# Sparse attention and a gated FFN on one core: the keys loaded first, a PSUM unit for zero matmuls, all early blocks in halves, a new order

## The chip, the cores and the metric

The kernel runs on one core of a Trainium2 chip. The metric is the device time of one execution in microseconds; lower is better. It is given as the median of several runs, and one execution more is taken with the hardware profiler.

## The reference

Four sequences of 768 tokens with 8 heads of 64 go through block-sparse attention (blocks of 32; a query block sees its neighbours, the first and last block, and three sampled blocks), and the result through a gated FFN of width 1536. Cut to what is computed:

```python
scores = (1 / np.sqrt(D)) * np.matmul(q, k.transpose(0, 1, 3, 2))
scores = np.where(mask, scores, -1000000000.0)       # mask: window, first/last, sampled blocks
attn = np.exp(scores - scores.max(-1, keepdims=True))
attn = attn / (attn.sum(-1, keepdims=True) + 1e-09)
x = np.matmul(attn, v)                               # -> 3072 tokens x 512
gate = 1.0 / (1.0 + np.exp(-(x @ w_gate)))
out = (gate * (x @ w_val)) @ w_out
```

## The kernel before

The work is cut into 12 units of 256 queries: three for each sequence (batch). A unit has four pairs of heads. For each pair there are three **score** steps (256 keys each): PE multiplies the transposed keys kT by the queries qT, two heads side by side in the two halves of its rows, ACT takes the exponential of the 128x1024 result into P, and for all units but the first DVE multiplies P by a 0/1 mask. In unit 0 the mask isn't ready as a tile in time; there a **bias** is added by extra matmuls, so a score step has eight matmuls instead of four. Then **PV**: 24 products of P and the values (with a column of ones for the sums), a reciprocal and a multiplication on DVE, and **xt**, the transpose of the result (units 0 and 1 on PE, the later ones by a transposing DMA on SP's queue).

The FFN follows by groups: units 0 to 3 each alone, then two at a time. A group has **F** blocks (x by w_gate and w_val into the two banks of one PSUM unit, tanh on ACT, the product on DVE into ht) and **y** parts (ht by w_out), a copy and a store. A group of one unit has six F blocks; each needs x from all four pairs and one of the six parts of w_gate and w_val.

PSUM is four units of two banks. Every task that writes PSUM takes a unit, and the order says which.

A block can be done in two ways. `whole` contracts 128 rows at a time. `turns` works with the two 64-row halves of the array side by side: in the first half-task the upper rows write bank 0 and the lower ones bank 1, in the second they change banks, and the second starts with a wait for the last matmul of the first. `WIDE = 2` makes PV and F whole in units 0 and 1. The closing blocks of the last unit (`y_last`) are whole in any case.

**The order.** Each piece of work is added to a list and gets a number; `ORDER`, written out by hand, says in which order they are issued, and each engine runs its own in that order. `30:2` is task 30 in PSUM unit 2; a letter (A or D) gives the copy to ACT or DVE; `215@30` issues load 215 after task 30 has run; `j3` is a pair of zero matmuls into unit 3, 64 rows by 512 columns each (L315). At the start of `ORDER` the numbers mean: 0 the block mask on DVE; 1 and 2 the bias, 3 and 4 the mask rows; 5 to 13 the casts, transposes and copies of pair 0's keys and queries; 15 to 18 transposes and copies of pair 1; 30 to 65 scores and PVs of unit 0; 66 to 73 the queries' later tiles; the F blocks of the first group begin with 126.

**Loads.** The first keys and queries come as float32 on SP's and ACT's queues (`first_heads`, L247) into a staging tile and are cast; the constants (identity and the mask's table) come on SP's queue, `e64` (which spreads block values over positions) by two loads. All else of batch 0 and the weights comes on POOL's queue, in the order of `FIRST`: k, q, v of the later pairs (k1 is the keys of pair 1; q1 the first queries of pair 1), then r0 to r3 (the later queries of the pairs) between w0 to w5 (parts of w_gate and w_val), at last o0 to o2 (w_out).

```python
nc.sync.dma_start(const, const_h.ap())
nc.scalar.dma_start(sbi, sampled_blocks)
first_heads(nc.sync, k32, k, 0, NT)
first_heads(nc.scalar, q32, q, 0, 2)
nc.gpsimd.dma_start(e64[0:NB], spread_h.ap())
nc.scalar.dma_start(e64[D : D + NB], spread_h.ap())
```

Of the kernel before, what the change touches and what calls it, by code (L numbers as in the profile page):

```python
# [21 lines left out]
NB = S // BLK  # L22
# [19 lines left out]
23D 25:3 27:2 37 26D 215@30 50:1 28D 46:3 51 82:2 48:0 83D 47 64:1 49 84:2 60:0 85D 65 38:3 29 61  # L42
56:2 39 66:1 57 42:0 67D 54:3 43D 52:1 165:0 53D 55 93:2 24 58:1 166 94 99:3 59 68:2 95:0 100 96D
181:1 69D 62:0 182 63D 78:3 102:2 162:0 79D 144@102 103 70:1 126:3 125@50 71D 183 163 164 111:1
127 119:2 131:0 120 128 167 112 104 138:3 122:2 132 145:1 123 133 121 139 124 169:0 146 140 147
72:2 170 86:3 159:1 73D 87 171 152:2 160 205:0 153 108:3 88 89:1 206 105@89 90 101 174:2 92@165
154 109 187@89 207 239:1 91 235@86 175 155:0 188:3 110 156 114@40 176 168@155 240 113 115:0 157
189 141:2 116 202:1 142 190 195:0 203 143 196 232:3 172:2 233 129:0 173 97:3 191:2 130 204 192A
193 98A 117:0 256 212:2 194 216 118A 213 184:3 177:0 217 178A 185 134:2 148:0 218 149D 135D 241
242:0 198:3 221A 252:2 214 199 136 179 219A 258 180 246:3 200 253 227 137 254 268:1 247 257 243  # L50
248 150 229:2 234 151 269 209:3 300:0 210 270 259 161 230 237 197 293:1 296:3 228 301 284:2 231
297 302 238 244 294 280:0 186 287:3 285 201@280 211 281 286 249:1 298 288 277:0 223:2 289 278 250
224 251 336:3 327:0 337 158@336 225 274 264:1 279 261:2 271:3 265 295 236 328 262 266 272 310:1
329 273 311 226 263 307:2 320:3 255 340 308 290 312 303:1 321 309 323:2 341 282 324 333:3 208 304
378@333 322 342 334 305 347:2 345A 343D 351:3 314:1 245@351 352 348 338 372:0 315 299@64 349 373
365:3 316 357@181 369 375:2 353 386:0 403@239 358:1 376 317 374 366 387 377 325 354:2 359 367 355
368 404:0 360 356 432:3 400:2 405 433 361 313@400 260 393:1 326@307 401 335 411:3 267@333 406 402
418:2 394 419 424@418 412 407 283@138 395 362:0 413 389:2 379:1 390 414 363 397:3 425:2 364 398
# [3 lines left out]
442:3 385 448 493:2 457A 451 455A 443 371 516:1 465 494 517 444 507:0 429 430 495 518 459:3 490:1  # L62
# [3 lines left out]
532:2 644:0 551 533 529:1 645 534 597:2 562 530 646 563 557 598 594:0 564 578 392@594 595 531  # L66
601:1 633@421 565D 567A 561@32 627:2 569:0 610 628 573:3 579@141 570 602 438@122 571 574 629
339@555 630:2 587:0 631 596 704@50 647:3 575 588 548@397 603 648 604 600@470 580:2 396 683@209 589
662:1 545:3 581 668@165 663 590 632 619:0 546 622:1 664 582 599 620 611:3 623 583 612 621 615:2
624 665:3 625 673:0 666 616 547 350 674 756:1 614@40 634:3 675 757 710 695 584:0 553 617 635 445  # L70
718@435 618 651:1 636 535@662 585 650@102 680:2 652 586 681 637 684:0 653 613 677:2 701:3 654 685
# [3 lines left out]
739:0 727 733 679 731 743:3 740 744 734 741 755 688:1 752 735A 722:0 728 689 737A 723 690 787:3  # L75
749:2 788 724 801:1 572 742 798:0 745 790:3 750 799 748 709 751 791 766:0 541 802 792 769:3 759
770 711 772:1 767 760 773 768 676 844:3 779:0 761 775:1 762A 764D 845 780 763 818:2 776 781 800
# [6 lines left out]
906 916 885 912 909A 921:1 913 974 946 922 924 927 923 907D 970:3 941:2 900 931 971 901:0 942 972  # L84
918:3 932 917 919 933 902 947:2 934D 954:3 936A 975 903 959:0 965:1 960 943 948 961 955 949 966
# [6 lines left out]
1067:0 1065 1081 1068 1085 1069 937 1066 1070 1086 935 1074 910 1075 1087 1076 1090D 1100:3 1091  # L92
1079D 1096:0 1077D 1078 1101 1080 1097 1102 1132:2 1103 1098 1088A 1108:3 1099 1089 1120:1 1109
1112:0 1110 1121 1111 1113 1122 1092:3 1123 1114 1124:1 1115 1133 1093 1104:0 1094 1125 1095 1105
1126 1134 1136:3 1127 1106 1135 1116:1 1107 1128:2 1117 1137 1118 1129 1119 1138 1140:0 1139 1130
1141 1131 1142 1150:1 1151 1152 1143 1153 1144 1154 1145 1160:3 1146A 1148D 1161 1147 1162 1149
1155:2 1163 1156 1164 1157 1158 1159
"""
GAP, PV_HALF, F_HALF, Y_ONE = 0.3, 0.36, 0.875, 0.216
WIDE = 2  # L100
# [20 lines left out]
class Plan:  # L121
# [13 lines left out]
    def run(self):  # L135
        done = set()
        for token in self.order:
            if token[0] == "j":
                self.idle(int(token[1:]))
# [15 lines left out]
def kernel(  # L155
# [46 lines left out]
    e64 = sing.tile([128, S], f16)  # L202
    nc.vector.memset(e64, 0.0)
# [47 lines left out]

    nc.sync.dma_start(const, const_h.ap())
# [32 lines left out]
    junk = sing.tile([128, 512], f16)  # L285
    nc.vector.memset(junk, 0.0)
# [816 lines left out]
```

## Time and profile before

| | us |
|---|---|
| median of 3 runs | 283.47 (283.11 to 285.92) |
| the profiled execution | 281.96 |
| its span, first to last instruction | 280.2 |
| PE busy in it | 272.4 (97%) |
| ACT / DVE / POOL busy | 192.1 / 187.9 / 47.4 |

PE is TensorE's matmuls, PEld its weight loads (they overlap with matmuls), DVE VectorE, ACT ScalarE, POOL GpSimd, SP SyncE. Timeline rows give the start, the duration, engine and line, what is written and read, shape and count, and in brackets the idle time before it with what ended it; neighbours of one kind are merged, and the duration of a merged row goes from its first start to its last end. Matmuls overlap: what one costs is seen from the start of the next, not from its duration. Rows of DMA issues give the size of one and the time from issue to landing.

### The profile page before, as it was taken

How to read it: one execution, taken by the hardware profiler on the slowest of the kernel's cores; microseconds unless marked ns; L12 is line 12 of the kernel's file. 1: busy time of each engine (PE TensorE's matmuls, PEld its weight loads, DVE VectorE, ACT ScalarE, POOL GpSimd, SP SyncE). 2: the span in 40 equal slices, each digit the busy share in tenths (PEclk: the TensorE clock that was granted, in tenths of full speed). 3: DMA queues.
4: the chain of work that ended last, by engine and by line, in shares of the span. 5: the costliest groups of instructions: out<-in, count | busy, mean ns of one | idle time of the engine just before them, and what ended most of it. 6: DMA issues, size and time to landing. Idle time of an engine off the chain costs nothing.

```text
span 280.2 us, 10875 instructions
## 1 busy us (share of the span) xinstructions
PE 272.4 (97%) x4889; PEld 186.1 (66%) x4889; DVE 187.9 (67%) x387; ACT 192.1 (69%) x239; POOL 47.4 (17%) x70
## 2 busy tenths in 40 slices
PE   5999999999999999999999999999999999999995
PEld 2677786777899799766555655666656667555543
DVE  4667894788887888688778746875664888142421
ACT  3798888699897878898668866578677683023301
POOL 8975441011531000082400000000000000000000
PEclk9799999999999999999999999999999999999999
DMA  7999999765589975279967330041100012440003
GB/s 148 184 195 196 200 205 202 110 127 87 77 110 150 206 129 126 40 106 188 125 115 162 68 97 2 12 133 50 30 2 0 6 21 65 117 180 2 0 5 147
DMA packets 56679, 28.92 MB, mean 103 GB/s; under 512 B 33044, under 2 KB 53676, under 8 KB 56632
## 3 DMA queue, kind: packets, MB, share of 16 engines
q0 software_dynamic: 21552, 13.93, 35.6%
q1 hardware_dynamic: 34592, 13.99, 22.7%
q8 instruction: 38, 0.62, 0.9%
q10 hardware_dynamic: 488, 0.30, 0.4%
q14 instruction: 9, 0.07, 0.1%
HBM read 28.47 MB, written 6.29 MB: 124 GB/s over the span
## 4 chain that ended last, share of the span: by engine, by line
PE 91%; DMA 3%; ACT 2%; DVE 2%; issue 1%; SPq 0%; DVEq 0%
PE m L338 89%; DMA xT<-x 2%; DMA e<-bb_spread 1%; ACT P L570 1%; PE m L456 1%; DVE ysb L833 1%; ACT ysb L831 0%; PE m L451 0%; DVE kT L282 0%; DVE mask L282 0%; ACT mask L280 0%; SPq L667 0%; PE m L397 0%; DVE x L616 0%; PE m L315 0%
## 5 line engine op out<-in xcount | busy, mean ns | idle before, releaser
L570 ACT ACTIVATE P<-m 128x1024 f16<-128x1024 f32 x144 | 142.5, 1025 | 31.3 <-PE m L338 27.3
L338 PE MATMUL m<-xT,wv 64*128 64x512 f16 (+2 forms) x672 | 136.1, 331 | 0.3 <-issue 0.3
L338 PE MATMUL m<-xT,wg 64*128 64x512 f16 (+2 forms) x672 | 135.9, 331 | 0.1
L576 DVE TENSOR_TENSOR P<-P,mask 128x1024 f16<-128x1024 f16 x132 | 86.7, 686 | 11.1 <-ACT P L570 10.8
L338 PEld LDWEIGHTS <-wg 64*128 64x128 f16 (+1 forms) x672 | 61.8, 94 | 20.5 <-issue 2.0
L338 PEld LDWEIGHTS <-wv 64*128 64x128 f16 (+1 forms) x672 | 61.8, 94 | 15.9 <-issue 0.3
L338 PE MATMUL m<-wo,ht 64*128 64x512 f16 (+2 forms) x564 | 70.7, 372 | 0.0
L765 DVE SCALAR_TENSOR_TENSOR ht<-th,m 128x512 f16<-128x512 f32 x72 | 49.0, 686 | 30.6 <-ACT th L762 29.6
L762 ACT ACTIVATE th<-m 128x512 f32<-128x512 f32 x72 | 42.7, 598 | 36.0 <-PE m L338 35.3
L338 PE MATMUL m<-qT,kT 64*128 64x256 f16 x576 | 54.0, 272 | 0.3 <-DVE ysb L833 0.2
L338 PEld LDWEIGHTS <-P 64*128 64x128 f16 (+1 forms) x2112 | 46.2, 94 | 9.0 <-issue 1.1
L338 PE MATMUL m<-vex,P 64*128 64x65 f16 (+1 forms) x2112 | 48.2, 190 | 0.0
L338 PEld LDWEIGHTS <-ht 64*128 64x128 f16 (+1 forms) x564 | 30.5, 94 | 21.6 <-issue 1.3
L338 PEld LDWEIGHTS <-kT 64*128 64x128 f16 x576 | 27.4, 95 | 13.0 <-issue 1.7
L220 POOL DMA_DIRECT2D v<-in_v_dram x16 | 11.4, 717 | 65.3 <-PE m L338 56.5
L616 DVE TENSOR_TENSOR x<-m,rz 128x256 f16<-128x256 f32 x48 | 20.4, 425 | 1.7
L615 DVE RECIPROCAL rz<-m 128x4 f32<-128x4 f32 x48 | 8.7, 180 | 17.9 <-PE m L338 16.4
L220 POOL DMA_DIRECT2D q<-in_q_dram x19 | 13.6, 723 | 12.1 <-PE m L338 11.1
L831 ACT ACTIVATE ysb<-m 128x512 f32<-128x512 f32 x13 | 7.5, 597 | 10.6 <-PE m L338 9.9
L833 DVE TENSOR_SCALAR ysb<-m 128x512 f32<-128x512 f32 x9 | 6.1, 688 | 11.8 <-ACT ysb L831 5.5
L220 POOL DMA_DIRECT2D k<-in_k_dram x15 | 10.8, 723 | 6.1 <-PE m L338 5.5
L338 PE MATMUL m<-bias,e 64*128 64x256 f16 x48 | 6.9, 301 | 0.3
(46 smaller groups left out, 69.7 us busy)
## 6 DMA issues: line engine op xcount, KB each, us to landing
out_dram<-ysb SPq DMA_DIRECT2D x23, 256.0 KB, 2.4
v<-in_v_dram POOLq DMA_DIRECT2D x16, 192.0 KB, 5.5
k<-in_k_dram POOLq DMA_DIRECT2D x15, 192.0 KB, 5.9
q<-in_q_dram POOLq DMA_DIRECT2D x12, 192.0 KB, 7.1
wg<-in_moe_w_gate_dram POOLq DMA_DIRECT2D x6, 256.0 KB, 8.6
wv<-in_moe_w_val_dram POOLq DMA_DIRECT2D x6, 256.0 KB, 8.9
wo<-in_moe_w_out_dram POOLq DMA_DIRECT2D x3, 512.0 KB, 12.8
xT<-x SPq DMA_TRANSPOSE x40, 3.2
```

Source lines behind the costliest of these rows:

```text
L220: return nc.gpsimd.dma_start(dst[:, h0:h1, t0:t1, :], src[b, h0:h1].rearrange("h (p t) d -> p h t d", t=NT)[:, :, t0:t1, :],)
L338: return nc.tensor.matmul(out, lhsT, rhs, start=start, stop=stop, skip_group_check=True).ins
L456: nc.tensor.transpose(out16[a * D : (a + 1) * D, h, i * D : (i + 1) * D], tile_[rows, a], ident[rows, rows],)
L570: nc.scalar.activation(self.pt.rearrange("a h i n -> a (h i n)"), both(self.bank).rearrange("a h n -> a (h n)"), AF.Exp, bias=0.0, scale=SCALE
L576: nc.vector.tensor_tensor(self.pt, self.pt, m.unsqueeze(1).broadcast_to([128, 2, 2, UQ]), op=ALU.mult,)
L615: nc.vector.reciprocal(rz, self.acc[:, :, :, D : D + 1])
L616: nc.vector.tensor_tensor(self.x16.rearrange("a s h d -> a h s d"), self.acc[:, :, :, 0:D], rz.broadcast_to([128, 2, 2, D]), op=ALU.mult,)
L762: nc.scalar.activation(th, both(bank)[:, 0, :], AF.Tanh, bias=0.0, scale=0.5)
L765: nc.vector.scalar_tensor_tensor(self.ht[:, tiles[0] : tiles[-1] + 1, :], in0=th.rearrange("a (f n) -> a f n", n=self.w), scalar=1.0, in1= ...
L831: nc.scalar.activation(ysb, both(bank)[:, s, :], AF.Copy, bias=0.0, scale=0.5)
L833: nc.vector.tensor_scalar(ysb, in0=both(bank)[:, s, :], scalar1=0.5, scalar2=None, op0=ALU.mult)
```

## The change

The order of the loads: the first keys go ahead of the constants on SP's queue, and `e64` comes on SP's queue (behind the constants) and on POOL's. The tile of zeros is smaller, cleared before `e64`, and read with a repeated axis; beside `j3` there is `j3s`, a pair of 128 columns, and the zero matmuls run on in unit 3 between the first real pieces. The block mask (task 0) is issued after the casts of the keys instead of ahead of everything, reads the sampled blocks without a cast, and reduces once into both places. `WIDE` and `WIDE_PV` are 0: PV and F of units 0 and 1 are in halves too, 20 tasks more (1185 for 1165), so the numbers are others. `EARLY` is 0, so the branch that it guards isn't taken. `ORDER` is another from first to last. In the new numbers, 15 to 18 are still pair 1's transposes and copies; 69, 71, 73 and 75 are the transposes of the later queries (r0 to r3) of pairs 0 to 3; 96 and 97 are unit 0's last PV; 93, 90, 113, 116, 104 are exponentials of unit 1; 131 is the first half of the first F block.

```diff
+EARLY = 0
 ORDER = """
-j3 j3 j3 j3 0 j3 j3 j3 11D 1:0 8A 3:1 5D 12:2 6:3 4A 7D 2 13A 80:3 106:1 9:0 30:2 107A 10D 81D
-15:1 31 34:0 16D j3 76:3 17:2 35 32:1 18D 77D 74:2 33 40:0 14 20:3 75D 41 44:1 21D 22:2 45 19 36:0
...
+j3 j3 j3 j3 j3 j3 j3 5A 8D j3 j3s j3s 0 j3s j3s 9:0 j3s j3s 11A 10D j3s 1:1 j3s j3s j3s 12:2 2 3:0
+13A 6:1 j3s 32:2 4D 7A 15:1 17:3 33 34:0 18D 16D 122:3 35 77:2 123D 30:1 78D 31 81:3 45:0 82D 22:2
+46 36:1 23D 41:3 37 20:2 21D 25:0 42 19 52:1 26D 56:2 53 47:3 14 49:0 57 38:1 48 27:2 50 28D 39
+51 63:2 58:3 24 64 83:0 40 84D 101:1 59 67:2 29 102A 69:0 60:3 68 70D 71:1 43:0 61 72A 44D 92:2
+89:0 62 93 112:1 54:3 55D 90 79:2 73:3 80D 113 115:0 74D 96:2 87:3 116 97 88D 103:1 98 104 65:3
+124:0 66D 99:2 146:3 125 100D 75:1 114 131:2 147 76D 106:0 117 127:1 132 107 126 194:3 128 138:0
...
-WIDE = 2
+WIDE, WIDE_PV = 0, 0
...
+    junk = sing.tile([128, 128], f16)
+    nc.vector.memset(junk, 0.0)
     nc.vector.memset(e64, 0.0)
...
+    first_heads(nc.sync, k32, k, 0, NT)
+    nc.scalar.dma_start(sbi, sampled_blocks)
     nc.sync.dma_start(const, const_h.ap())
-    nc.scalar.dma_start(sbi, sampled_blocks)
-    first_heads(nc.sync, k32, k, 0, NT)
     first_heads(nc.scalar, q32, q, 0, 2)
-    nc.gpsimd.dma_start(e64[0:NB], spread_h.ap())
-    nc.scalar.dma_start(e64[D : D + NB], spread_h.ap())
+    nc.sync.dma_start(e64[0:NB], spread_h.ap())
+    nc.gpsimd.dma_start(e64[D : D + NB], spread_h.ap())
...
     def mask_blocks(eng):
-        sbf = sing.tile([NB, 3], f32, name="sbf")
-        nc.vector.tensor_copy(sbf, sbi.bitcast(u16)[:, 0:12:4])
...
-            sbf.unsqueeze(1).broadcast_to([NB, NB, 3]),
+            sbi.bitcast(u16)[:, 0:12:4].unsqueeze(1).broadcast_to([NB, NB, 3]),
...
-        for o in (0, D):
-            nc.vector.tensor_reduce(
-                mb16[0:NB, o : o + NB], mc, axis=mybir.AxisListType.X, op=ALU.max
-            )
+        nc.vector.tensor_reduce(
+            mb16[0:NB].rearrange("a (o n) -> a o n", n=D)[:, :, 0:NB],
+            mc.unsqueeze(1).broadcast_to([NB, 2, NB, 4]),
...
-    def idle(unit):
+    def idle(unit, kind):
+        n = 1 if kind == "s" else 4
         for i in range(2):
+            rows = slice(i * D, (i + 1) * D)
             nc.tensor.matmul(
-                units_ps[unit][:, i, :],
-                junk[i * D : (i + 1) * D, 0:128],
-                junk[i * D : (i + 1) * D, :],
+                units_ps[unit][:, i, 0 : n * 128].rearrange("a (x n) -> a x n", n=128),
+                junk[rows],
+                junk[rows].unsqueeze(1).broadcast_to([D, n, 128]),
...
-            if self.n < WIDE:
+            if self.n < WIDE_PV:
...
+            if self.g == 0 and j < EARLY:
...
+            elif self.ns[-1] < WIDE:
```

More of the change, by code (lines that the diff above doesn't have):

```diff
@@ L45 @@
[L45 to L56, printed above, removed]
@@ new lines @@
+89:0 62 93 112:1 54:3 55D 90 79:2 73:3 80D 113 115:0 74D 96:2 87:3 116 97 88D 103:1 98 104 65:3
+124:0 66D 99:2 146:3 125 100D 75:1 114 131:2 147 76D 106:0 117 127:1 132 107 126 194:3 128 138:0
+108 94 133 135:1 129 139 195 134 136 140 153:3 137 91 179:2 196 164:1 180 148 165 105 161:1 141
+154 181 162 182 186:0 155 172:2 168:1 156 173 249@172 187 152@56 149:3 174 169 178@45 150 201:2
+170 109@89 188 256:1 151 95@34 190:3 202 166 191A 257 200@63 216:3 189 118@161 203 119:0 215@146
+243:1 204 217 244 274 120 163 197:2 157:1 218 198 229@197 158D 121 183:1 130@172 142:0 212:2 184
@@ new lines @@
+143D 213 245 246:0 230 185 247 175:2 207 205:1 231 206D 208 176 199 223:0 85:1 232 159 224 86D 160
+284:2 251 233A 177 235A 226:1 209:0 225 285 227 144 219:3 272 286 319:1 145 248 210 241 220 228
+320 252 287 267:0 221 321 275 264:2 322 253:3 268 254 242 211 265 214 269 260:1 192 266 193 237:3
+261 270 258 273 238 262 280:2 301:0 239 281 263 291 294:3 255 327:2 295 110:1 302 240 111D 328
+288:3 271 277:1 250 282 289 278 305:2 290 303 330:1 309 312:3 306 331 304 296 347:0 307 313 315:1
+308 348 167@315 279 316 297:2 349 332 298 317 343:3 340:1 360 259@343 344 299 283@58 356:2 171 341
@@ new lines @@
+361 314 346@297 323:3 329 357 353:1 362 345 354 409:2 324 363D 365A 423@409 385:1 325 410 333@30
+374:0 355 337 371:3 386 375 222 342 334:2 372 399:0 276 358 387 335 420:3 388 400 421 318@420 336
+382:1 300@409 401 438:2 367:3 412@67 439 402 383 368 398@103 431:0 369 444@47 384 417:2 455:3
+377@103 432 376 456 359@164 338 378:1 422 433 339 445:3 418 434 350 440 392:0 466:2 379 393 373
[3 rows of a table added]
+404 429 454 477A 501 311 496:3 430 475A 502 536:2 479:1 449 370 537 565:0 488 497 566 293 480
[4 rows of a table added]
+589:3 583 629 580 596:1 577 590 597 650:0 584 591 651 616 631:3 607:1 585D 587A 604:0 416 632
@@ new lines @@
+664:2 598 688@327 608 665 724@52 605 621:3 653@103 609 606 568@374 610 647:2 600:0 648 666 581@149
+700:1 622 633 555@209 701 595 599@507 601 623 639:2 624 602 642:1 603 617:3 640 618 703@617 735:0
+643 641 620@438 736 649 661 682:2 635:3 670@510 619 683 458@115 476 652 671:0 644 634@112 667:2
+636 645 668 702 654:1 637 718:2 638 672 719 684 721:3 655 673 573 722 674 675:2 612 656 711:0 720
+613 716 676 657 723 685:3 689:1 677 680 574 686 630 712 678 625 693:3 730 690 713 560 714 611
+704:2 691 465 725:0 626 738@312 588 692 586 694 669 697:1 705 698 695 726 687 715 706 739:3 707
@@ new lines @@
+727 731 708:1 728 773:2 740 592 774 561 737 709 732:0 658:2 710 733 741 729 792:1 734 807:0 659
+793 646 752 660 808 776:1 696 679 753 699 777 746:2 662 754 747 763:0 759:1 755D 757A 742:2 760
+764 769:3 761 838:0 772 835:1 743 839 770 744 836 778 789:0 762 771 790 837 849:2 717 818:1 765
+779 850 749:0 756 780 851 750 781 819 751 810:2 802:0 775 811 791 795:1 784A 748 803 782A 785 840
[6 rows of a table added]
+925 889 911 916 990:0 964:1 917 926 991 923 934 931:2 965 947 941:0 905 963 927A 932 979:1 942 933
+980 937 944 943 929A 958:2 928 982:1 938:3 959 983 951 960 939 984 1039:1 1036:2 952 1037 940 953
@@ L98 @@
+1040 1024:3 971:2 954A 1041 985:1 956A 955 972 1025 1067:0 986 973 1068 966 989 1013:3 987 1049:2
[6 rows of a table added]
+1095 1096 1107 1097A 1112:3 1108A 1099A 1120:2 1110A 1113 1111 1098 1132:1 1114 1109 1100 1144:0
[3 rows of a table added]
+1171 1168A 1166D 1169 1172 1167 1180:1 1173 1181 1182 1174 1183 1184
 """
 GAP, PV_HALF, F_HALF, Y_ONE = 0.3, 0.36, 0.875, 0.216
-WIDE = 2
+WIDE, WIDE_PV = 0, 0
 TOK = (np.arange(S) % 128) * NT + np.arange(S) // 128
@@ L138, in run @@
             if token[0] == "j":
-                self.idle(int(token[1:]))
+                self.idle(int(token[1]), token[2:])
                 continue
@@ L284 @@
     nc.vector.memset(mb16, 0.0)
-    junk = sing.tile([128, 512], f16)
-    nc.vector.memset(junk, 0.0)
     for r in range(2):
@@ L295, in mask_blocks @@
             mc[:, :, 1:4],
[L296 removed]
+            sbi.bitcast(u16)[:, 0:12:4].unsqueeze(1).broadcast_to([NB, NB, 3]),
             op=ALU.is_equal,
         )
[L299 to L302 removed]
+        nc.vector.tensor_reduce(
+            mb16[0:NB].rearrange("a (o n) -> a o n", n=D)[:, :, 0:NB],
+            mc.unsqueeze(1).broadcast_to([NB, 2, NB, 4]),
+            axis=mybir.AxisListType.X,
+            op=ALU.max,
+        )
     units_ps = [ps.tile([128, 2, 512], f32, name=f"m{i}") for i in range(4)]
@@ L355, in turns, with whole @@
                 )
-    def whole(mms, bank):
+    def whole(mms, bank, begins=True, ends=True):
         for n, job in enumerate(mms):
@@ L361, in whole @@
                 out, lhsT, rhs = job(g, slice(0, 128))
-                bank.last = tiled(out, lhsT, rhs, n == 0, n == len(mms) - 1)
+                bank.last = tiled(
+                    out, lhsT, rhs, begins and n == 0, ends and n == len(mms) - 1
+                )
     copies = {}
@@ L740, in f, with half @@
             tiles = range(self.per * j, self.per * (j + 1))
-            def half(first):
+            def half(first, cs=range(4)):
                 def go(eng):
@@ L745, in go @@
                     for o, f in enumerate(tiles):
-                        for c in range(4):
+                        for c in cs:
                             mms.append(
@@ L754, in go @@
                     if first is None:
-                        whole(mms, bank)
+                        whole(mms, bank, cs[0] == 0, cs[-1] == 3)
                     else:
@@ L774, in f @@
             deps = xdone[self.g] + before("ht", self.g)
-            if self.ns[-1] < WIDE:
+            if self.g == 0 and j < EARLY:
+                a = plan.add(
+                    [(PE, 1.5 * F_HALF)],
+                    half(None, range(3)),
+                    xdone[0][:3] + before("ht", 0),
+                    take=bank,
+                    ops=12 * self.per,
+                    wide=True,
+                )
+                a = plan.add(
+                    [(PE, 0.5 * F_HALF)],
+                    half(None, range(3, 4)),
+                    [a] + xdone[0][3:],
+                    ops=4 * self.per,
+                    wide=True,
+                )
+            elif self.ns[-1] < WIDE:
                 a = plan.add(
```

23 lines of the change are left out of this document (removed), and 43 rows, old and new, of the table ORDER.

## The prediction

> **What bounds the kernel now.** I read the page first: busy time per engine, then the forty slices.
>
> ```profile
> PE 272.4 (97%) x4889; PEld 186.1 (66%) x4889; DVE 187.9 (67%) x387; ACT 192.1 (69%) x239; POOL 47.4 (17%) x70
> PE   5999999999999999999999999999999999999995
> PEclk9799999999999999999999999999999999999999
> GB/s 148 184 195 196 200 205 202 110 127 87 77 110 150 206 129 126 40 106 188 125 115 162 68 97 2 12 133 50 30 2 0 6 21 65 117 180 2 0 5 147
> ```
>
> TensorE is the bound. Its clock dips in the second slice alone, and for the first seven slices (49 us) the DMA engines move a flat 184 to 205 GB/s, so what is loaded there comes as fast as it can. Then the windows (PE, PEld, DVE, ACT, POOL busy, then the clock):
>
> ```profile
> 5.02:8.43 3.41, 2.00 (x55) 1.60 (x54) 2.09 (x6) 2.60 (x5) 3.35 (x6) 1.00 1.20 154
> 8.43:11.84 3.41, 3.41 (x51) 1.98 (x38) 2.11 (x6) 2.12 (x3) 3.14 (x5) 0.50 1.38 185
> 22.08:25.02 2.94, 2.71 (x70) 1.72 (x66) 2.51 (x7) 2.74 (x4) 2.19 (x3) 1.00 1.45 195
> 62.50:250.00 187.50, 186.82 (x3730) 129.39 (x3730) 134.46 (x271) 135.63 (x166) 18.33 (x26) 1.00 0.49 89
> 277.00:280.20 3.20, 0.00 (x0) 0.00 (x0) 0.42 (x1) 0.00 (x0) 0.00 (x0) 1.00 0.29 102
> ```
>
> A window in which PE was busy 2.00 of 3.41 us is followed by one at half clock. From 62.5 to 250 us PE idles 0.7 us in 187.5, so a new order has little to win there. The change can act in two places: until the first F block, and in what a block of matmuls costs beside its columns.
>
> The head, from the timeline by engine: zero matmuls, the casts of the first keys, mask and bias, the exponentials, the last two PE blocks before the end of the head.
>
> ```profile
> 1.66 3.17 PE L315 MATMUL m<-junk 64*128 64x512 f16 x14 [1.66 <-DVE junk L286]
> 5.28 0.62 ACT L280 CAST qp<-kp 128x512 f16<-128x512 f32 x1 [3.26 <-DMA kp<-in_k_dram]
> 3.01 0.22 DVE L293 TENSOR_TENSOR const<-const,sbf 24x72 f32<-24x72 f32 x1
> 3.26 0.40 DVE L300 TENSOR_REDUCE mb<-const 24x24 f16<-24x96 f32 x2
> 6.65 0.41 DVE L411 TENSOR_SCALAR bias<-m 128x256 f16<-128x256 f32 x1
> 8.08 1.02 ACT L570 ACTIVATE P<-m 128x1024 f16<-128x1024 f32 x1
> 9.55 1.02 ACT L570 ACTIVATE P<-m 128x1024 f16<-128x1024 f32 x1 [0.45 <-PE m L338]
> 11.41 7.67 ACT L570 ACTIVATE P<-m 128x1024 f16<-128x1024 f32 x8 [0.84 <-DVE mask L282]
> 19.39 1.96 ACT L570 ACTIVATE P<-m 128x1024 f16<-128x1024 f32 x2 [0.31 <-PE m L338]
> 24.77 0.32 PE L456 MATMUL m<-const,q 64*64 64x64 f16 x16 [0.15 <-ACT P L570]
> 25.02 0.28 PE L338 MATMUL m<-xT,wg 128*128 128x256 f16 x1
> ```
>
> Unit 0 has twelve exponentials. They run one behind the other on ACT, eight in 7.67 us (0.96 each), and end at 19.39 + 1.96 = 21.35. The first F block starts at 25.02. So the head is bound by ACT and by what arrives, the rest by PE.
>
> **The change, the head.** First the keys: their load moves from SP's second place to its first.
>
> ```profile
> 0.74 0.35 SPq L252 DMA_DIRECT2D const<-bb_const  x1
> 1.15 0.50 SPq L247 DMA_DIRECT2D kp<-in_k_dram  x1
> 2.96 0.73 POOL L220 DMA_DIRECT2D q<-in_q_dram  x1
> q<-in_q_dram POOLq DMA_DIRECT2D x1, 64.0 KB, 5.1
> 14.21 0.71 POOL L220 DMA_DIRECT2D q<-in_q_dram  x1
> q<-in_q_dram POOLq DMA_DIRECT2D x1, 128.0 KB, 8.2
> 17.34 0.70 POOL L220 DMA_DIRECT2D q<-in_q_dram  x1 [0.24 <-DMA wg<-in_moe_w_gate_dram]
> q<-in_q_dram POOLq DMA_DIRECT2D x1, 128.0 KB, 8.4
> 27.98 0.74 POOL L235 DMA_DIRECT2D wo<-in_moe_w_out_dram  x1 [1.15 <-DMA wg<-in_moe_w_gate_dram]
> wo<-in_moe_w_out_dram POOLq DMA_DIRECT2D x1, 512.0 KB, 13.5
> ```
>
> Issue 0.41 us earlier lets the keys land at 5.25 - 0.4 = 4.85. But the mask, which was ready at 3.66, now stands behind the keys' cast on DVE and needs the constants, which come after the keys. Behind it wait the copy of the keys' transpose and the bias. The sum: 4.85, cast 0.62, mask 0.22 + 0.3 (two reductions made one; the u16 cast is gone), the keys' copy 0.4 (as the bias, an estimate), bias 0.41, making 6.8. In the old run from the bias' end (7.06) to the exponential was 1.0; so the first one starts near 7.6 instead of 8.08. At worst the mask takes back the 0.4 and it stays at 8.1; at best the keys land another 0.4 earlier.
>
> That gain is hidden for the second exponential. In the new order the PE does the transposes of k and q of pair 1 (tasks 15 and 17) ahead of the second score (34). That q was issued at 2.96 and takes 5.1: 8.1. Then 0.3 of transposes and the score, and the second exponential starts at about 9.1 (old 9.55). Ten more at 0.96, a mask copy that the order now gives to ACT ahead of the last of the twelve (0.6) and 0.5 of gaps: unit 0's twelfth ends near 9.1 + 1.0 + 9.6 + 0.6 + 0.5 = 20.8, 0.55 ahead of the old 21.35.
>
> What follows is against the change. The transposes of q's later tiles of pairs 2 and 3 (tasks 73 and 75) stood at 24.77 and after the fourth F block; now both stand **ahead of the first F block** (131). Their loads land at 14.21 + 8.2 = 22.4 and 17.34 + 8.4 = 25.7, and by the flat GB/s these move little. Task 75 also takes PSUM unit 1, which the exponential of unit 1, pair 0, third step (104) frees. Ahead of it on ACT stand a copy of 0.4 and four exponentials: 20.8 + 0.4 + 5 x 0.96 + 0.1 = 26.1. Either way 75 can't run before 25.7 to 26.1; with its 0.25 (24.77 to 25.02) the first F block starts near **26.4, 1.4 us later** than now. Bounds: 25.0 if loads and ACT both come 1.4 earlier, 28 if the second half of the head falls to half clock.
>
> By then more is done: two more scores and one more set of transposes than at 25.02 (seven scores of unit 1 or 2 against five, the same masks, all four PVs). At 0.22 and 0.25 that is 0.7 us of PE. Just after the start ACT is still two exponentials behind and holds the units that task 194, the second F block and its third want: 0.4 us of PE waiting, an estimate. Net of the head: +1.4 - 0.7 + 0.4 = **+1.1 us**.
>
> The zero matmuls fill PE, which the order leaves idle anyhow; 14 of them took 3.17. Ahead of the first transposes now stand 16 of the same (3.6) and 8 of a quarter of the columns (0.45), which start near 1.1, when the smaller junk tile is cleared, and end near 5.1; the keys' cast ends at 5.5. Cost 0 as long as it does; if the keys land at 4.2, the zeros delay the first transposes by some 0.3.
>
> **The change, whole blocks.** Timeline of PE around whole and halved blocks:
>
> ```profile
> 26.87 0.61 PE L338 MATMUL m<-qT,kT 64*128 64x256 f16 x8
> 27.41 0.28 PE L338 MATMUL m<-xT,wg 128*128 128x256 f16 x1
> 33.98 0.90 PE L338 MATMUL m<-vex,P 128*128 128x65 f16 x24
> 34.82 0.39 PE L338 MATMUL m<-qT,kT 64*128 64x256 f16 x4
> 35.05 0.53 PE L338 MATMUL m<-vex,P 64*128 64x65 f16 x24
> 35.41 0.60 PE L338 MATMUL m<-qT,kT 64*128 64x256 f16 x8
> 35.85 0.53 PE L338 MATMUL m<-vex,P 64*128 64x65 f16 x24
> 87.40 0.27 PE L338 MATMUL m<-xT,wv 64*128 64x256 f16 x1
> 88.27 0.40 PE L338 MATMUL m<-qT,kT 64*128 64x256 f16 x4
> ```
>
> A whole F takes 25.02 to 26.87, 1.85. The eight score matmuls ahead of the next whole F take 0.54 (26.87 to 27.41), ahead of a halved PV 0.44 (35.41 to 35.85): 0.10 for going in. So 1.95 alone, against two halves of 0.87 (87.40 to 88.27), 1.74: **0.21 saved each time PE goes in and out**. A whole PV takes 0.84 + 0.10, two halves 2 x 0.36: again 0.21. The twelve F blocks and four PVs of unit 1 stand in the old order in 11 such runs (F 0; 1; 2 and 3; 4; 5 with a PV; three of the second group; three alone; two runs of PVs): 11 x 0.21 = **-2.3 us**, all on PE's path. The PVs of unit 0 lie in the head, under ACT, and give nothing. The price of the halves is a wait between the first and the second half, which change banks, 20 times. The new order puts another block between most of them; I take 0, bounded by 0.10 each, +2.0.
>
> **Orders anew, the end.** The third part of w_out lands at 27.98 + 13.5 = 41.5. The new order wants it after twelve F halves and two y parts (as many columns) at 0.87, ten scores, six PV halves: 12.2 + 2.2 + 2.2 + 0.5 = 17.1 after the first F, 43.5: 2 us of room. For batch 1 the tightest transposing load has a little less room than now; for the rest I take 0, with -0.7 and +0.7 (the idle time above) as bounds. At the end ACT's copy and queue replace DVE's and SP's: 0.
>
> **Sum.** +1.1 - 2.3 = -1.2 us. The profiled execution took 281.96 (span 280.2 and 1.76 around it): 280.8. The runs' median is 283.47, 1.5 above it, so the forecast for the median is **282.3**.
>
> **Rivals.** (1) *The head hands over in time.* If the loads land 1 us earlier without the constants ahead and ACT runs without gaps, F starts at 25.0: the +1.4 and the 0.4 fall away and 0.7 stays: -3.0, **280.5**. For it: ACT's gaps of 0.45 and 0.84 came from PE at half clock. Against: 25.7 is a landing at a rate that is flat.
>
> (2) *The halves cost what the whole blocks did.* 20 waits of 0.10: -1.2 + 2.0 = +0.8, **284.3**. Against: the halves at 35.05 and 35.85 show no gap. [...]
>
> (3) *Slower: the clock falls ahead of F.* Place: 18.7 to 26.4, where PE now waits for two loads and for ACT. It has some 4 us of work in 7.7. It decides once PE's busy share in one window falls to the 59% (2.00 of 3.41) that preceded the half clock; 92% (2.71 of 2.94) did not. A half clock that covers the start of F costs half of 3.41, 1.7; two in a row 3.4: +0.5 to +2.2, taken as **285.0** (+1.5). Against: half-clock work itself fills the window, and F comes next. [...]
>
> (4) *It doesn't fill what it says*: the quarter-size zeros are too few to lift the window after 5.02 over 59%, and the clock still halves. That is within the forecast, as loads hide it.
>
> **How the numbers follow.** Forecast 0.52, rival 1 0.22, rival 2 0.13, rival 3 0.13. One per cent, 2.83 us, is about what a measurement of this kernel can tell from no change: faster below 280.6, slower above 286.3. Rival 1 lies just beyond, with a little of the forecast: faster 0.23. Half-clock windows in two stages or a late load on top of rival 3: slower 0.10. Same 0.67. The forecast's own range is 281 to 283.5. The range goes from 279.6 (rival 1 and -0.7 and the better keys) to 285.2 (rival 3).
>
> **What would show it.** Right: keys' cast near 4.9; first exponential 7.3 to 8.0, second 8.8 to 9.4; PE idle before the transposes of q at 25 to 26; first F at 25.8 to 27; no 128-row matmuls before the last stage; score blocks of four at 0.22 throughout. Wrong: F starting under 25 or beyond 28, a half clock after 20 us, gaps of 0.1 between halves.

## The result, and the profile after

The changed kernel takes 286.12 us (median of 16 runs, 285.26 to 287.67), the kernel before in the same sessions 283.38 (16 runs, 280.38 to 285.92). The ratio is 1.0111, with a 95% interval of 1.0087 to 1.0136: slower by 1.1%, where 282.3 was forecast and the range ended at 285.2. The profiled execution took 285.94, with a span of 284.1 against 280.2.

The page after: busy time and instructions of the engines, the clock by slices, and the queue whose packets fit PE's program.

```profile
PE 272.0 (96%) x5295; PEld 192.6 (68%) x5295; DVE 185.4 (65%) x381; ACT 192.5 (68%) x243; POOL 47.3 (17%) x70
PEclk9997999999999999999999999999999999999999
q8 instruction: 41, 0.67, 1.0%
```

PE is busy as long as before (272.0 against 272.4), in 5295 matmuls instead of 4889; the 3.9 us more of span are idle time. The dip of the clock has moved from the second slice to the fourth. By its counts the last line is PE's program, in 41 packets of 16 KB (0.67 MB). A matmul with its weight load is two instructions (5295 of each), so 2 x 5295 in 41 packets makes 258 instructions in each; the kernel before had 38 packets (0.62 MB) for 2 x 4889, 257 in each.

The head and two later gaps, from the timeline by engine: first exponential, then PE.

```profile
6.90 1.02 ACT L577 ACTIVATE P<-m 128x1024 f16<-128x1024 f32 x1 [0.18 <-PE m L343]
19.54 0.28 PE L343 MATMUL m<-bias,e 64*128 64x256 f16 x2 [0.45 <-issue]
23.91 0.21 PE L343 MATMUL m<-vex,P 64*128 64x65 f16 x2
25.74 0.79 PE L343 MATMUL m<-vex,P 64*128 64x65 f16 x22 [1.62 <-issue]
29.22 0.28 PE L343 MATMUL m<-xT,wg 64*128 64x256 f16 x1
37.85 0.27 PE L343 MATMUL m<-xT,wv 64*128 64x256 f16 x1 [0.63 <-issue]
98.61 0.82 PE L343 MATMUL m<-wo,ht 64*128 64x512 f16 x6 [1.45 <-issue]
```

The start is better than forecast: first exponential at 6.90 (8.08 before). But in the middle of a PV half, with its inputs there, PE stops after two matmuls, from 23.91 to 25.74. "issue" means that it waits for nothing that the profile shows. The first F starts at 29.22, where 25.02 stood before and 26.4 in the forecast. The waits of PE that are "issue" (us in all, how many, the longest), after and then before:

```profile
PE m L343 <- issue: 4.2, 4, 1.6
```

```profile
PE m L338 <- issue: 0.3, 1, 0.3
```

Four such gaps, 4.2 us, against one of 0.3. Now windows of the changed kernel; the first two end where PE goes on after a gap, and the third ends as many instructions later (columns: the stretch; its length; busy time and instructions of PE, PEld, DVE, ACT, POOL; clock; DMA share; GB/s). Then come three windows of 3.41 us, as long as the half clock lasts here and lasted before (8.43 to 11.84): two around the second gap, and the one that holds the last gap.

```profile
0.00:19.53 19.53, 15.60 (x351) 10.58 (x352) 10.54 (x29) 13.32 (x17) 15.30 (x26) 1.00 1.16 175
19.53:25.73 6.20, 3.75 (x128) 2.78 (x128) 2.64 (x7) 5.79 (x8) 4.42 (x6) 0.98 1.45 196
25.73:31.92 6.19, 6.06 (x128) 4.67 (x128) 4.22 (x10) 4.02 (x5) 2.22 (x3) 0.74 1.45 197
22.07:25.48 3.41, 1.22 (x30) 0.81 (x28) 1.43 (x4) 3.40 (x4) 2.22 (x3) 1.00 1.45 197
25.48:28.89 3.41, 3.15 (x68) 2.24 (x67) 1.85 (x6) 0.99 (x2) 2.22 (x3) 0.50 1.45 196
97.16:100.57 3.41, 1.96 (x25) 1.23 (x24) 2.30 (x5) 1.57 (x2) 0.00 (x0) 1.00 0.88 173
```

From the first gap's end to the second's PE executes 128 matmuls and 128 weight loads, 256 instructions, about as many as one packet holds, in 6.20 us while the DMA engines move 196 GB/s; the next 256 take 6.19 at 197 GB/s, and those after them, up to the end of the third gap (37.84), 5.92 at 206. The second gap also takes 1.36 us out of the window from 22.07 to 25.48, and short waits for ACT (0.29 and 0.38) and DVE (0.15) take more. PE is left busy for 1.22 of 3.41 us, and the next 3.41 us run at half clock, just ahead of F. The last gap leaves 1.96 of 3.41, and the clock behind it stays full.

### The profile page after: what moved, and what is told of

It reads as the page before. It is cut to its first block, busy times and chain, and to the rows that moved or that the text cites. A ratio compares the mean times of both kernels' runs of the same rounds, so it can differ in the third digit from the quotient of the medians.

```text
span 284.1 us, 11693 instructions
## 1 busy us (share of the span) xinstructions
PE 272.0 (96%) x5295; PEld 192.6 (68%) x5295; DVE 185.4 (65%) x381; ACT 192.5 (68%) x243; POOL 47.3 (17%) x70
## 4 chain that ended last, share of the span: by engine, by line
PE 91%; issue 2%; DMA 2%; POOL 2%; ACT 1%; DVE 0%; ACTq 0%
PE m L343 90%; DMA k<-in_k_dram 2%; ACT P L577 1%; PE m L463 1%; POOL k L225 1%; POOL q L225 0%; POOL v L225 0%; DVE ysb L856 0%; POOL e L262 0%; PE m L458 0%; ACT ysb L854 0%; DVE e L208 0%; ACT ysb L897 0%; DVE junk L207 0%; ACTq L577 0%
## 5 line engine op out<-in xcount | busy, mean ns | idle before, releaser
L343 PE MATMUL m<-xT,wv 64*128 64x256 f16 (+1 forms) x768 | 138.3, 322 | 0.6 <-issue 0.6
L343 PE MATMUL m<-xT,wg 64*128 64x256 f16 (+1 forms) x768 | 137.9, 322 | 0.3
L343 PEld LDWEIGHTS <-wg 64*128 64x128 f16 x768 | 69.8, 94 | 17.4 <-issue 0.8
L343 PEld LDWEIGHTS <-wv 64*128 64x128 f16 x768 | 69.7, 94 | 15.7 <-issue 0.3
L769 ACT ACTIVATE th<-m 128x512 f32<-128x512 f32 x72 | 42.8, 599 | 30.4 <-PE m L343 26.4
L343 PEld LDWEIGHTS <-P 64*128 64x128 f16 x2304 | 48.0, 95 | 9.9 <-issue 1.7
L343 PE MATMUL m<-vex,P 64*128 64x65 f16 x2304 | 50.1, 191 | 1.6 <-issue 1.6
L343 PEld LDWEIGHTS <-kT 64*128 64x128 f16 x576 | 29.0, 94 | 12.1 <-issue 0.8
L854 ACT ACTIVATE ysb<-m 128x512 f32<-128x512 f32 x18 | 10.1, 600 | 19.8 <-PE m L343 18.3
L287 DVE CAST mask<-m 128x512 f16<-128x512 f32 x8 | 5.3, 687 | 3.0 <-PE m L343 2.9
L343 PE MATMUL m<-bias,e 64*128 64x256 f16 x48 | 5.8, 271 | 0.7 <-issue 0.5
```

The costliest lines, as they stand in the source:

```text
L287: nc.vector.tensor_copy(dst, src)
L343: return nc.tensor.matmul(out, lhsT, rhs, start=start, stop=stop, skip_group_check=True).ins
L769: nc.scalar.activation(th, both(bank)[:, 0, :], AF.Tanh, bias=0.0, scale=0.5)
L854: nc.scalar.activation(ysb, both(bank)[:, s, :], AF.Copy, bias=0.0, scale=0.5)
```

## The experiments

**Theory A, instruction fetch**, worked out from these counts and windows: PE gets its program in blocks of 256 instructions ("program blocks" below); beside loads of 196 GB/s such a block can't be had faster than every 6.2 us (6.20 and 6.19 above), and the change (halves have twice the matmuls of whole blocks, and there are more zero matmuls) makes PE use them up faster. **Theory B, order**: what the new order puts ahead of F makes it late. **Theory C**: the halves wait where they change banks.

**1. The changed order with whole blocks.**

```diff
-            if first is None:
-                whole(mms, self.bank)
+            if first is None or self.n < 2:      # and in F: self.ns[-1] < 2
+                if first is not False:
+                    whole(mms, self.bank)
...
```

> The changed kernel, its order and head kept, but the PV and F blocks of the first two units run whole (128 rows) where the first half stood. This takes 8 x 24 + 12 x 16 = 384 matmuls out of PE's stream (5295 to 4911) and no work. Theory A, instruction fetch: the gaps in the changed kernel's trace for which PE waits on nothing (1.82 us at 23.9, 0.90 at 36.9, 1.82 at 96.8) come because PE runs through its instructions faster than they are brought; with fewer instructions they shrink to under 1 us in all, no window after 20 us falls to half clock, the first F starts at 26 to 27 (29.2 in the changed kernel), and the time is 286.1 - 2.8 (head) - 2.7 (later gaps) + 2.3 (going in and out of whole blocks) = 283 (282 to 284). Theory B, order: the new order's prep of q ahead of F and its waits for loads and ACT make the late F; then F stays near 29 with a half clock ahead of it, and the time is 286.1 + 2.3 = 288. Theory C, the halves wait at their bank change: time falls by up to 2 but F stays at 29, 286.

290.14 us, ratio to before 1.0235 (1.0177 to 1.0294): none of the times expected.

```profile
0.00:27.49 27.49, 22.03 (x468) 15.25 (x468) 14.96 (x42) 20.66 (x25) 21.14 (x33) 1.00 1.24 178
27.49 0.28 PE L343 MATMUL m<-xT,wg 128*128 128x256 f16 x1
37.35 1.02 ACT L577 ACTIVATE P<-m 128x1024 f16<-128x1024 f32 x1 [3.74 <-PE m L343]
PE m L343 <- ACT P L577: 3.9, 6, 1.1
```

The head is as A says: full clock up to the first F, and that at 27.49 instead of 29.22. Behind it whole F blocks run back to back in places laid out for halves with scores between them, and ACT gets nothing for up to 3.74 us. PE in its turn waits for ACT, 3.9 us in all (0.7 in the changed kernel), and its fetch gaps are 1.9 instead of 4.2. So a whole block can't simply be put where a half stood, and the run bears on the head alone.

**2. The order of before with halves.**

```diff
             if first is None:
-                whole(mms, self.bank)            # and so in F
+                turns(mms, self.bank, True)
+                turns(mms, self.bank, False)
```

> The kernel before, its order and head kept, with the 8 PV and 12 F blocks of the first two units cut in halves that run one behind the other in the place of the whole block: 384 matmuls more, no work more. Theory A (fetch): gaps without a wait appear in the first 50 us, 1 to 3 us in all, and eat the 2.3 that the halves save: 283 to 285 (before 283.4). Theory B (order): no such gaps, the -2.3 comes through: 281 to 282. Theory C (bank change): gaps of 0.1 between the first and the second half of each block, 20 x 0.1 = 2.0: 283.1, without gaps over 0.5.

291.77 us, 1.0303 (1.0245 to 1.0361).

```profile
0.00:22.38 22.38, 17.63 (x351) 11.04 (x352) 11.96 (x34) 14.23 (x16) 17.63 (x29) 1.00 1.20 178
22.38:28.57 6.19, 2.95 (x128) 2.47 (x128) 1.77 (x6) 3.07 (x3) 3.63 (x6) 1.00 1.45 196
28.58 0.23 PE L451 MATMUL m<-const,x 64*128 64x64 f16 x4 [3.12 <-issue]
29.84:33.25 3.41, 3.34 (x46) 1.83 (x43) 2.30 (x4) 2.16 (x3) 1.79 (x3) 0.50 1.40 201
37.37 0.27 PE L338 MATMUL m<-xT,wg 64*128 64x256 f16 x1
37.48 0.61 PE L338 MATMUL m<-xT,wv 64*128 64x256 f16 x2
37.82 0.28 PE L338 MATMUL m<-xT,wg 64*128 64x256 f16 x1
```

In another order, at other work and another time, the gap again stands behind 351 matmuls and 352 weight loads, and the next 128 and 128 later; the block again takes 6.19; a half clock follows. A is right and the size was underrated: 3.12 us in one gap, 5.9 in all. C is right here too: pairs of matmuls follow each other by 0.11 us (37.37 to 37.48), but from the first half's last pair (37.48) to the second's first (37.82) it takes 0.34, so 0.23 for this change. The run has twenty such changes; at 0.23 that would be 4.6 us, an estimate, so A and C share what this run lost. The kernel puts a wait at each change, and the 0.23 is the price with this wait; whether it could be left out no run here shows. The changed order puts other blocks between the halves, and between its halves PE shows only one step over 0.23, 0.41 at the end of a program block (102.89).

**3. The transposes of q behind F.**

```diff
-... 100D 75:1 114 131:2 147 76D 106:0 ...
+... 100D 114 131:2 147 106:0 ...
-... 91 179:2 196 164:1 ...
+... 91 179:2 196 75:1 76D 164:1 ...
```

> The changed kernel with the transposes of pair 3's later q tiles and their copy moved from ahead of the first F block to behind the fourth. Theory B (order): those transposes, which wait for a load and for a PSUM unit, make F late; without them F starts at 25.5 to 26.5, no half clock, 283.5. Theory A (fetch): the gap of 1.8 us at 23.9 stands ahead of them and stays; the clock still falls; F moves only by the 0.3 that they wait and by their own time at half clock (0.5), to about 28.4, and the time is 285.3.

286.47 us, 1.0113 (1.0076 to 1.0150), the changed kernel's own ratio.

```profile
25.48 0.51 PE L343 MATMUL m<-vex,P 64*128 64x65 f16 x22 [1.62 <-issue]
28.12 0.37 PE L343 MATMUL m<-xT,wg 64*128 64x256 f16 x1
```

The gap stays, and F comes near the 28.4 that A expected, though the time is 1.2 above A's 285.3. F starts 1.1 us earlier, and nothing is won: B falls for this step, and a first F that is early because work was put behind it is no gain.

**4. The same columns in more instructions.**

```diff
-j3 j3 j3 j3 j3 j3 j3 5A 8D ...
+j3m j3m j3m j3m j3m j3 j3 5A 8D ...
+        if kind == "m":      # eight pairs of 64 columns for one pair of 512
...
```

> The changed kernel with the first five pairs of zero matmuls (512 columns) cut into eight pairs of 64 columns each: the same columns, 70 matmuls more, which is 140 PE instructions (a weight load and a matmul each), all ahead of the first keys. Theory A (fetch in blocks of 256 instructions): the gaps, which stand at PE instructions 706, 962, 1474, 4290 and 4546 of the changed kernel (multiples of 256 apart), move to work that lies 140 instructions earlier: 962 becomes what is now number 822 (21 us) and 4290 what is now 4150 (about 94 us); the 1.8 at 23.9 vanishes or shrinks below 1, so that F may start 1 to 2.5 us earlier although instructions were added: 284 to 286. Theory B (order) and C (bank change): nothing moves after 8 us, gap and half clock stay where they are, 286.

289.63 us, 1.0234 (1.0174 to 1.0294): 3.5 us more than the changed kernel, for the same columns of zeros in 70 matmuls more.

```profile
0.00:16.95 16.95, 13.70 (x351) 10.64 (x352) 8.52 (x22) 11.53 (x14) 13.94 (x24) 1.00 1.10 169
16.95:23.15 6.20, 3.79 (x128) 3.01 (x128) 2.71 (x8) 3.35 (x4) 4.31 (x6) 1.00 1.45 196
23.15:29.35 6.20, 5.52 (x128) 4.29 (x128) 3.70 (x10) 4.91 (x6) 3.70 (x5) 0.57 1.45 196
23.16 0.22 PE L474 MATMUL m<-const,q 64*64 64x64 f16 x2 [2.07 <-issue]
```

The place was forecast rightly (again 351 and 352, then 128 and 128, with 6.20 us to a block), the sign of the time wrongly: the gaps came to 6.8 us instead of 4.2, and the half clock to 6.83 us instead of 3.41. Where a gap stands goes by the number of the instruction in these three kernels (351 and 352), not by the work at it.

**5. Whole PVs in unit 0 alone.**

```diff
-            if first is None:
+            if first is None or self.n < 1:
...
```

> The changed kernel with only the four PVs of unit 0 whole again, where their first half stood; its F blocks and the PVs of unit 1 stay in halves. 96 matmuls (192 PE instructions) fewer, all ahead of the first F. Theory A (fetch: a block of 256 PE instructions can't be used up in less than 6.2 us while the loads fill the DMA queues): the head is that of the run with whole blocks, no gap without a wait before F, no half clock, first F at 27.5; behind F the halves keep their 2.3, but all later gaps stand at other work, 192 instructions later. 286.1 - 1.7 = 284.4, with 1 either way for where the later gaps fall. If the slower time of the run with whole blocks came from the whole PVs in the head and not from the whole F blocks behind it, this run is slow too: 288.

287.00 us, 1.0116 (1.0091 to 1.0141), not 284.4.

```profile
25.11 0.69 DVE L287 CAST mask<-m 128x512 f16<-128x512 f32 x1 [0.99 <-PE m L343]
25.86 0.23 PE L458 MATMUL m<-const,x 64*128 64x64 f16 x4 [0.57 <-DVE mask L287]
25.93 0.42 DVE L624 TENSOR_TENSOR x<-m,rz 128x256 f16<-128x256 f32 x1
26.27 0.71 DVE L287 COPY xT<-m 128x256 f16<-128x256 f16 x2
27.18 0.28 PE L343 MATMUL m<-xT,wg 64*128 64x256 f16 x1
0.00:95.47 95.47, 86.04 (x2013) 71.09 (x2014) 71.24 (x159) 74.14 (x90) 38.21 (x57) 1.00 1.10 158
95.48 0.39 PE L343 MATMUL m<-wo,ht 64*128 64x512 f16 x2 [3.09 <-issue]
95.97:99.38 3.41, 3.41 (x25) 1.81 (x22) 0.69 (x1) 2.15 (x3) 0.00 (x0) 0.50 0.80 125
```

The head is mended (no gap, full clock, F at 27.18), and the loss comes back 65 us later: 3.09 us at the end of another block, and a half clock behind it. The first rows show what F waits for when fetch is out of the way: the last PV's normalisation stands on DVE behind a mask copy of 0.69 (PE itself idles 0.57 for that copy), and the copies of xT behind it.

**6 and 7. The start alone.** The order and whole blocks of before with the new loads, junk tile and mask; then the changed kernel's first steps too (the edit is written against the changed kernel).

```diff
-WIDE, WIDE_PV = 0, 0
+WIDE, WIDE_PV = 2, 2
 ORDER = """                       # the order of before; in the second run it begins:
+j3 j3 j3 j3 j3 j3 j3 5A 8D j3 j3s j3s 0 j3s j3s 9:0 j3s j3s 11A 10D j3s 1:1 j3s j3s j3s 12:2 2 3:0
+13A 6:1 j3s 4D 7A 80:3 106:1 30:2 107A 81D
...
```

> The kernel before, its order, its whole blocks and its number of zero matmuls kept, with the changed kernel's loads at the start (keys ahead of the constants, spread on SP and POOL), its junk tile and its shorter mask computation. One part of the change alone. Keys land at about 4.1 instead of 5.25, first exponential at 7.0 to 7.5 (8.08); PE's instruction stream is the same, so no gaps without a wait. The start of F hangs on the loads of q, so it moves by 0 to -0.5: 283.0 (282.5 to 283.6).

> As the run with the new loads, and the changed kernel's first steps too (38 zero matmuls instead of 14, keys cast first), ahead of the rest of the order of before with whole blocks. The half clock at 8.43 to 11.84 goes, the first exponential starts at 6.9. Theory A (fetch): 48 PE instructions more shift the blocks, whole blocks use them up slowly, so gaps of under 0.5 in all; first F at 24 to 25; 282.5 (281.5 to 283.5). Theory B (the new order as a whole makes F late, not the start): the same here. If the zero fill itself costs (it delays the first transposes), F starts past 25.5 and the time is 284.

The new loads alone: 283.30 us, 0.9987 (0.9960 to 1.0013), no difference. With the new first steps: **281.59 us, 0.9923 (0.9898 to 0.9949)**, faster than both kernels. First the one, from the timeline of ACT, then the first exponentials, a window and the first F of the other.

```profile
4.19 0.62 ACT L284 CAST qp<-kp 128x512 f16<-128x512 f32 x1 [2.17 <-DMA kp<-in_k_dram]
8.73 1.02 ACT L576 ACTIVATE P<-m 128x1024 f16<-128x1024 f32 x1 [0.48 <-PE m L342]
```

```profile
8.42 6.86 ACT L577 ACTIVATE P<-m 128x1024 f16<-128x1024 f32 x7
8.43:11.84 3.41, 3.14 (x90) 2.28 (x91) 2.36 (x7) 3.29 (x5) 3.38 (x6) 1.00 1.33 175
25.50 0.28 PE L343 MATMUL m<-xT,wg 128*128 128x256 f16 x1
```

Keys that are cast at 4.19 instead of 5.28 give no earlier exponential by themselves, and with the new first steps it starts at 8.42, not at the expected 6.9. With these steps and their zeros the stretch from 8.43 to 11.84 runs at full clock and executes 90 matmuls (0.50 and 51 before; 1.00 and 58 with the new loads alone). Where the 0.8% is won the profile doesn't show: the first F is no earlier (25.50), and from it to the end of the span it takes 280.6 - 25.50 = 255.1 us, as before (280.2 - 25.02 = 255.2). The profiled execution was the slowest of the five (282.36).

**8. Few loads.** Only w0 and the first part of w_out are loaded; the other blocks read these. The changed kernel by itself, then both kernels side by side.

```diff
         if name[0] == "w":
-            load_w(j)
+            if j == 0:                      # and so for load_wo
+                load_w(j)
-    (wg, wv)[g][rows, c, f * 128 : (f + 1) * 128]
+    (wg, wv)[g][rows, c, f % 2 * 128 : f % 2 * 128 + 128]      # and wo[rows, f % 4, :]
```

> The changed kernel with the loads of w1 to w5 and of the second and third part of w_out left out; the blocks that want them read w0 and the first part instead, so the output is not the reference's. PE's instructions are the same in number and order, and all waits but those for loads. Theory A (fetch is slow because the loads hold the DMA queues): the gaps at PE instructions 962 and 1474 vanish although the same 256 instructions are used up as fast; a block may then take 3 to 4 us; F starts at 25 to 26.5, full clock after 20 us, 281 to 282. If the gaps are PE's own (a fixed cost at these places, whatever the loads), 1.8 at 962 and 0.9 at 1474 stay, and time falls by less than 2.

> The kernel before with the loads of w1 to w5 and of two parts of w_out left out, as in the changed kernel's run with few loads (281.4). A control: its fetch gaps were only 0.3, so Theory A says that it gains little from them, only what it waits for data at the first F: 282 to 283, and the changed kernel with few loads is faster than it by the 1 that the prediction's sum gave. If lighter DMA traffic helps both alike, this run comes to 279 and fetch does not explain the difference between the two.

> The changed kernel with few loads again, timed beside the kernel before with few loads. Theory A: 281 to 282, 0.5 to 1.5 below that one.

The changed kernel by itself took 281.36; side by side it takes **281.76** (ratio to the unaltered kernel before 0.9966, 0.9940 to 0.9993) and the kernel before **282.97** (0.9999, 0.9974 to 1.0024). First the changed kernel with few loads, then the kernel before with few loads.

```profile
0.00:19.84 19.84, 15.52 (x351) 10.58 (x352) 10.60 (x29) 13.20 (x16) 13.03 (x22) 1.00 1.14 172
19.84:24.40 4.56, 3.72 (x128) 2.80 (x128) 2.54 (x7) 4.44 (x7) 0.00 (x0) 1.00 0.62 103
PE m L345 <- issue: 0.3, 1, 0.3
27.13 0.28 PE L345 MATMUL m<-xT,wg 64*128 64x256 f16 x1
```

```profile
26.21 0.28 PE L340 MATMUL m<-xT,wg 128*128 128x256 f16 x1
```

With the DMA engines at 103 GB/s the very program block that took 6.20 us takes 4.56, and the gap of 1.62 is gone, with the same instructions in the same order. Lighter loads take 4.4 us off the changed kernel (286.12 to 281.76) and nothing off the other. It is not that PE waits less for its data: its waits for k and q are 2.3 us here and were 1.6. This is what A said and B and C did not. Without the fetch gaps the changed kernel is 1.2 us below the kernel before, the forecast's own difference. The two intervals overlap a little, and in the profiled spans it is 2.1 (279.6 against 281.7), so that it is just 1.2 is partly luck.

**9. Fewer instructions at the start.**

```diff
-j3 j3 j3 j3 j3 j3 j3 5A 8D j3 j3s j3s 0 j3s j3s 9:0 j3s j3s 11A 10D j3s 1:1 j3s j3s j3s 12:2 2 3:0
+j3 j3 j3 j3 j3 j3 j3 5A 8D j3 j3s 0 j3s 9:0 11A 10D 1:1 j3s 12:2 2 3:0
...
-        for i in range(2):                  # a pair of 64-row zeros
...
+        # one zero of 128 rows; the short ones three times as long
...
```

> The kernel with whole PVs in unit 0 (287.0), with the zero matmuls at the start written shorter: each pair of 64-row zeros becomes one of 128 rows, and of the eleven short ones four are left, three times as long. That is 52 PE instructions fewer at the very start and nothing else. Theory A (fetch): the block that ends at PE instruction 4034 (gap 3.47 at 92.0, and a half clock behind it) now ends 52 instructions later in the work, where PE takes longer over it: gaps at the instruction numbers 194 + 256 n as ever, but under 1.5 us in all after 60 us, no half clock at 96, 283 to 284. If that gap belongs to the work at 92 us (a late transposing DMA, say) and not to the instruction count, it stays there and the time stays 287.

> The changed kernel with the same shorter zeros, 52 PE instructions fewer and nothing else. Theory A: worked out from the changed kernel's own instruction times with 6.2 us as the least for a block under load, the gaps come to as much as before (about 5 us), at the same instruction numbers 706, 962, 1474, 4546 but at other work: 285 to 287. If fewer zeros are themselves the gain, 283.

With whole PVs in unit 0: 283.96 us, 1.0027 (1.0000 to 1.0053), 3 below the run that differs from it by 52 zero-matmul instructions. On the changed kernel: 287.99, 1.0180 (1.0122 to 1.0238), above the 285 to 287 expected; its gaps come to 5.4 us instead of 4.2. A row of each profile with its gap:

```profile
0.00:96.45 96.45, 88.97 (x2013) 72.01 (x2014) 72.45 (x162) 77.00 (x93) 38.16 (x57) 1.00 1.10 157
96.46 0.82 PE L341 MATMUL m<-wo,ht 64*128 64x512 f16 x6 [2.05 <-issue]
```

```profile
0.00:21.62 21.62, 17.01 (x351) 10.55 (x352) 11.01 (x30) 14.77 (x18) 17.25 (x28) 1.00 1.17 174
21.63 0.45 PE L341 MATMUL m<-vex,P 64*128 64x65 f16 x18 [1.94 <-issue]
```

Gaps stand at the same counts, 2013 and 2014, 351 and 352, at work 52 instructions further on. The time followed the forecast in the first run, but its profile still shows a gap of 2.05 where under 1.5 in all was expected, and a half clock; that execution took 285.8, the slowest of ten from 282.7, so it may not be the usual one. How often a program block at this place is late stays open, and so does whether a transfer at 90 to 96 us holds it up.

## Why the prediction was wrong, step by step

- **Keys and exponentials: right in direction, too careful.** First exponential 6.90 (7.6 forecast). Single executions differ here: it starts at 6.90 to 7.30 in the five profiles with just this start (the changed kernel and runs 1, 3, 5 and 8), at 8.08 to 9.19 in the three with the old one (the kernel before and runs 2 and 8). The keys' place alone does not do it (8.73 with the new loads), nor do the new first steps in the order of before (8.42): the early start is of the new order as a whole.
- **Zero matmuls, "cost 0": right in itself.** From 8.43 to 11.84 the clock was 0.50 in the kernel before, 1.00 with the new loads and first steps, but 1.00 with the new loads alone too; that the zeros keep it is not shown. With both the order of before was 0.8% faster. But each zero is two PE instructions, and that had no row in the sum.
- **First F at 26.4: wrong by 2.8.** It started at 29.22. Without a fetch gap ahead of it it starts at 26.94 to 27.49 (four runs): 0.5 to 1.1 more than forecast. The step followed loads and ACT only and left out DVE's mask copy ahead of the last PV's normalisation; PE idles 0.57 us for it in run 5, and the rest of the difference wasn't traced. The other 2 us are fetch and the half clock behind it. That task 75 ahead of F would cost 1.4 is not borne out: moved away, it gave no time.
- **Halves, -2.3: right as far as it can be seen.** With few loads the stretch from F to the end of the profiled span is 279.6 - 27.13 = 252.5 in the changed kernel and 281.7 - 26.21 = 255.5 in the other (255.1 to 255.7 in the four profiles with the order of before and whole blocks). That is -3.0, where the forecast had -2.3, the 0.7 of work already done and 0.4 of waiting, -2.6; the terms were not measured one by one.
- **Bank change taken as 0: right for this order**, and 0.23 each where halves stand back to back, not the 0.10 of the bound.
- **The step that failed** is the one that costed halves at columns and waits. They also double the instructions for the same columns, and the sum had no term for bringing them. By the run with few loads it is worth 284.1 - 279.6 = 4.5 us of span: 29.22 - 27.13 = 2.1 ahead of F, and (284.1 - 29.22) - 252.5 = 2.4 behind it. So where the sum had -1.2, the profiled spans have -0.6 without the gaps (279.6 against 280.2) and +3.9 with them; the medians have +2.7.
- **Rival 3** (a half clock ahead of F, 285.0) had the place: 36% of a window, below its 59%. Its threshold doesn't hold: the window at 97.16, with 57%, was no busier than that one and kept the clock, as did one of 56% in run 4 (1.91 of 3.42 us, 95.75 to 99.17). So the busy share alone doesn't decide. Its reason was mostly another: of the window's idle time 0.67 was waiting for ACT, as it said, but 1.36 was for PE's program. That its price comes near the 286.1 is luck, as 2.4 of the 4.5 us lie behind F.
- **The other rivals** did not come: F nowhere started near rival 1's 25.0 in the new order, the halves did not wait as in rival 2, and the clock held through the start, against rival 4. Two of the prediction's own signs of being wrong did come, F beyond 28 and a half clock after 20 us.
- It could have been asked of the old profile: 2 x 4889 instructions in 38 packets, and 196 GB/s of loads in the head. Its one gap was of 0.3 us; those of the changed kernel and the runs were of 0.3 to 3.1 us.

## What to carry to other kernels

Count instructions as well as columns: where PE uses up 256 instructions in less time than they need to arrive beside the loads (6.2 us here at 196 GB/s), a cheaper block made of more instructions need not be cheaper. Here fetch showed as a gap with no wait that returned behind 351 matmuls and 352 weight loads in four kernels; shift the program by a few dozen instructions and see whether the gap moves to other work, or lighten the loads and see whether it goes (here at 103 GB/s, from 1.62 us to none). And a change that bundles a better start with a new order should be run in parts: here the start alone was worth 0.8%, and the rest took it away.

## What was not expected of the hardware

Beside loads of 196 GB/s a packet of PE's program came at least 3.8 us after PE had gone on behind the gap before. In the changed kernel PE went on at 19.54, and stood still again ahead of 25.74, 128 matmuls and 128 weight loads later. The DMA queues (packets, MB, share of 16 engines) from 19.54 to 23.30:

```profile
q0 software_dynamic: 1490, 0.74, 145.2%
```

And from 23.30 to 25.73:

```profile
q0 software_dynamic: 935, 0.46, 142.5%
q8 instruction: 1, 0.02, 2.5%
```

In the first part the loads alone move; the one instruction packet comes after 23.30, and PE goes on at 25.74. When the packet is asked for, and what holds it until then, no run shows. The same 6.2 us in all came back in three kernels under 196 GB/s (6.20 here, 6.19 in run 2, 6.20 in run 4). The other surprise is how much can follow: the gap of 1.62, with 0.8 of short waits in the same window, was followed by 3.41 us at half clock, while with few loads PE was busy for 2.66 of 3.41 us at the same work (22.62 to 26.03) and the clock stayed full (1.00).
